# Weight conversion in fewer steps, keys and queries loaded as pairs of rows, division ahead of the transposes, and a new opening order, in a kernel of windowed attention and a gated feed-forward layer

## The chip, the cores and the metric

The kernel runs on one core of one Trainium2 chip. The metric is the time of one execution in device microseconds (us): a median of 659.19 over three runs (658.7 to 659.53) for the kernel before.

## The reference

Attention over 4 batches, 8 heads, 768 positions and 64 numbers per head, then a gated feed-forward layer without an activation over 3072 tokens (512 to 1536 and back). Weights arrive as 64-bit floats.

```python
k_sum = k.reshape(B, H, nb, 32, D).max(axis=3)            # 24 block summaries per head
v_sum = v.reshape(B, H, nb, 32, D).mean(axis=3)
scores_l = scale * q @ k.T, kept where |i - j| < 16        # else -1e9
scores_s = scale * q @ k_sum.T + log(32)
a = softmax(concat([scores_l, scores_s]))                  # sum + 1e-9 in the divisor
x = a @ concat([v, v_sum])                                 # heads side by side: 3072 x 512
out = ((x @ w_a) * (x @ w_b)) @ w_out
```

## The kernel before, in words

**Tiling.** Queries go in groups of 128 rows; a group's scores are a window of 96 keys and 24 block summaries for each half of 64 queries, 120 columns per head, four pairs of heads in one PSUM bank and two banks (h = 0, 1) per group. Groups are gathered into units: units 0 and 1 are two groups each, unit 2 two more, the later ones three. `attention` and `first_attention` make `x` of a unit; `item` runs one slice f of 128 columns of the hidden layer for a unit: `up` (x times w_a and w_b, L1110), the gate, `down` (times w_out, L1232). There are 12 slices. For slices 0, 1 and 11, units 0 and 1 run apart with 256 columns per product; for slices 2 to 10 they run together with 512. x, the gate's result and the weights are each kept as a high part and a remainder in the fp32r format, so `up` takes 12 products per matrix and `down` 3 per group.

**Weights.** `convert` (L401) turns two parts of 512 columns x 128 rows of doubles (w_a, w_b or w_out of a slice) into fp32 and then into high and low. Per part: ACT scales the high words into PSUM (L424), DVE shifts them into `f` (L432), DVE cuts the exponent out (L439), DVE multiplies the low words by it into `p` (L445); ACT casts `f` to the high part (L477), POOL subtracts that from `f` (L482), POOL adds `p` (L488). 36 parts in all, in places of two parts in one operation where the scratch allows.

**The first four groups** (`first_attention`, units 0 and 1) are special. Keys and queries are loaded with rows on partitions (`heads`, runs of 64 floats) and turned by TensorE with `turn` (L507, four transposes); the mask and the log are added by TensorE before the scores (`masks`, L695: four products of 480 columns against the identity); the softmax runs on PSUM; the division is folded into the transposes: DVE builds a diagonal of reciprocals (L786) and `turned` multiplies each 120 x 128 block by it (L807). Later groups use DVE for masks and transposes.

**Order.** Every operation is recorded with `work.add` and gets an index; `emit` issues them by priority and an assumed duration, but the table `ORDER` fixes for each engine the order of the indices that it lists. Each engine runs its list strictly in order. SP's list is the queue of loads. `SPIN` lists 16 products against the identity whose results nobody reads (L1338); the table places them on PE.

Of the kernel before, what the change touches and what calls it, by code (L numbers as in the profile page):

```python
# [25 lines left out]
        2638 2639 13 2640 5 2641 1 2642 2643 21 2644 17 9 2645 75 57 55 77 58 78 2646-2648 96 98  # L26
        2649-2651 111 100 113 121 102 141 123 104 106 124 143 151 2652 153 154 2653 115 145 173
        171 542 543 180 175 550 178 548 182 549 555 557 556 558 565 563 564 572 570 573 571 582
        583 580 578 581 579 588 590 354 591-593 602 589 600 598 603 599 601 612 610 611 613 608
        609 622 618 623 620 619 621 632 630 628 633 629 631 642 643 640 638 641 639 650 648 510  # L30
        652 673 653 649 651 662 660 658 661 682 659 667 679 687 668 688 940 941 948 946 947 793
        955 953 954 962 960 849 961 967-969 976 974 975 983 903 981 829 982 990 997 988 989 1004
        995 996 883 1002 1003 1046 1009 1011 1018 1010 937 1016 1017 1023 1024 1186 1187 1194
        1195 1192 1193 1202 1200 1201 1097 1203 1210 1208 1209 1211 1218 1216 1217 1219
    """,
    "ACT": """
# [8 lines left out]
        806 809 958 802 963 965 970 972 857 977 855 854 862-864 861 865 979 856 689 984 858 986  # L45
# [3 lines left out]
    """,  # L49
    "DVE": """  # L50
        7 3 15 23 19 11 195 59 60 80 79 196 65 72 66 73 67 74 197 199 85 86 200 87 92 93 201 94
        209-211 213 126 214 223 215 224 125 225 227 138 228 139 156 131 155 132 140 133 168 229
# [25 lines left out]
    """,
    "SP": """
# [20 lines left out]
    ("h1", 512), ("h1", 128), ("h1", 64), ("h1", 64), ("h1", 256), ("h1", 256), ("h1",  # L100
    128), ("h1", 128), ("h1", 256), ("h1", 256), ("h1", 256), ("h1", 256), ("h1", 256),
    ("h1", 256), ("h1", 256), ("h1", 128)
# [76 lines left out]
def attention_moe(  # L179
# [193 lines left out]
    raws, homes = {}, {}  # L373

    def load_part(i, rank):
# [7 lines left out]
        def fn():  # L383
            if j not in raws:
                raws[j] = wp.tile([P, 2048], I32, tag=f"W{j}", name=f"raw{j}")
            dst = raws[j][:, i % 2 * 1024 : (i % 2 + 1) * 1024]
# [14 lines left out]
    def convert(j):  # L401
        rank = CONVERT + j / 6
# [10 lines left out]
        cols = [[slice(x * CV, (x + 1) * CV) for x in xs] for _, *xs in places]  # L413
        fx, px = [[spaces[places[h][0]][:, cols[h][x]] for h in range(2)] for x in range(2)]
        fk, pk = [[f"{places[h][0]}.{places[h][1 + x]}" for h in range(2)] for x in range(2)]
        spans = [(h,) for h in range(2)] if single else [(0, 1)]

        def scale(h):
            high = raws[j][:, 2 * h * CV : 2 * (h + 1) * CV].rearrange("p (n t) -> p n t", t=2)
            nc.scalar.activation(  # L424
                bank["c0"], high[:, :, 1].bitcast(F32), AF.Prelu, scale=2.0**-112, alpha=-(2.0**32)
            )
# [474 lines left out]
    def first_attention():  # L901
# [82 lines left out]
        for t in range(2):  # L984
            begin(t, f"h{t}")
# [389 lines left out]
```

## Time and profile before

| what | value |
|---|---|
| median of three runs | 659.19 us (658.7, 659.19, 659.53 in order of size) |
| span of the profiled execution, first to last instruction | 656.9 us |
| median less span: what lies around the span | 2.3 us |
| busy: PE / weight loads / DVE / ACT / POOL | 647.7 / 599.3 / 409.9 / 250.8 / 187.8 us |
| HBM read, written | 47.41 MB, 6.44 MB |
| mean granted TensorE clock | 0.999 |

For the profiled execution itself the profile gives the span alone; its own time is taken as the span and the 2.3 us around it. How to read it: "busy" adds up the time in which an engine had an instruction running, and a TensorE product counts until its results have drained. Its successor starts before that, so the price of a product in a stream is the distance from its start to the next one's, and the duration printed for a merged row is longer than its price by the drain of its last product.

### The profile page before, as it was taken

How to read it: one execution, taken by the hardware profiler on the slowest of the kernel's cores; microseconds unless marked ns; L12 is line 12 of the kernel's file. 1: busy time of each engine (PE TensorE's matmuls, PEld its weight loads, DVE VectorE, ACT ScalarE, POOL GpSimd, SP SyncE). 2: the span in 40 equal slices, each digit the busy share in tenths (PEclk: the TensorE clock that was granted, in tenths of full speed). 3: DMA queues.
4: the chain of work that ended last, by engine and by line, in shares of the span. 5: the costliest groups of instructions: out<-in, count | busy, mean ns of one | idle time of the engine just before them, and what ended most of it. 6: DMA issues, size and time to landing. Idle time of an engine off the chain costs nothing.

```text
span 656.9 us, 12984 instructions
## 1 busy us (share of the span) xinstructions
PE 647.7 (99%) x4943; PEld 599.3 (91%) x4943; DVE 409.9 (62%) x857; ACT 250.8 (38%) x749; POOL 187.8 (29%) x246
## 2 busy tenths in 40 slices
PE   8899999999999999999999999999999999999997
PEld 6699888899989999999999999999999999999997
DVE  3899999997786784666767846667652531122212
ACT  4997676523443441433333313343321411121111
POOL 6498999847333440111010101110100100000000
PEclk9999999999999999999999999999999999999999
DMA  9998666353443443322112422221100200010001
GB/s 218 277 286 243 229 188 173 79 118 105 128 92 78 112 95 57 71 82 44 39 39 52 84 42 43 41 82 35 25 1 1 71 1 1 0 49 1 0 1 49
DMA packets 158198, 54.71 MB, mean 83 GB/s; under 512 B 135736, under 2 KB 151352, under 8 KB 158136
## 3 DMA queue, kind: packets, MB, share of 16 engines
q1 hardware_dynamic: 157992, 53.75, 33.9%
q8 instruction: 39, 0.64, 0.4%
q14 instruction: 23, 0.19, 0.1%
q10 hardware_dynamic: 144, 0.13, 0.1%
HBM read 47.41 MB, written 6.44 MB: 82 GB/s over the span
## 4 chain that ended last, share of the span: by engine, by line
PE 89%; DMA 6%; SPq 2%; ACT 1%; issue 1%; POOL 0%; DVE 0%; DVEq 0%
PE h L1110 54%; PE o L1232 27%; PE c L708 3%; PE o L856 3%; SPq L357 2%; DMA raw<-in_moe_w_out_dram 1%; DMA space<-in_v_dram 1%; DMA raw<-in_moe_w_b_dram 1%; DMA raw<-in_moe_w_a_dram 1%; DMA space<-in_q_dram 1%; DMA qin<-in_q_dram 1%; SPq L389 1%; PE c L1110 1%; POOL space L482 0%; PE c L856 0%
## 5 line engine op out<-in xcount | busy, mean ns | idle before, releaser
L1110 PE MATMUL h<-x,w 128*128 128x384 f32 (+2 forms) x2064 | 389.1, 321 | 0.0
L1110 PEld LDWEIGHTS h<-x,w 128*128 128x128 f32 x2064 | 331.3, 190 | 10.5 <-issue 0.6
L1232 PE MATMUL o<-w,gh 128*128 128x512 f32 x534 | 131.7, 382 | 0.0
L1217 DVE TENSOR_TENSOR h<-h,g 128x384 f32<-128x384 f32 x71 | 40.2, 566 | 136.4 <-PE h L1110 128.8
L1219 ACT CAST gh<-h 128x384 fp32r<-128x384 f32 x71 | 34.0, 478 | 204.6 <-DVE h L1217 202.0
L1232 PEld LDWEIGHTS o<-w,gh 128*128 128x128 f32 x534 | 97.6, 189 | 12.2 <-issue 1.6
L840 DVE STREAM_TRANSPOSE pt<-s 32x256 f32<-32x256 f32 x228 | 99.4, 436 | 13.0 <-POOL s L794 8.3
L794 POOL TENSOR_TENSOR s<-s,nml 128x480 f32<-128x480 f32 x40 | 39.4, 987 | 220.2 <-DVE nml L779 218.1
L1110 PE MATMUL h<-late,w 128*128 128x384 f32 x288 | 93.9, 326 | 0.0
L759 ACT ACTIVATE s<-s,nml 128x120 f32<-128x120 f32 x160 | 61.3, 386 | 38.0 <-DVE nml L745 37.8
L1232 PE MATMUL o<-w,gl 128*128 128x512 f32 x231 | 63.3, 381 | 0.0
L1110 PEld LDWEIGHTS h<-late,w 128*128 128x128 f32 x288 | 54.4, 189 | 0.9
L1222 DVE TENSOR_TENSOR gl<-h,gh 128x384 fp32r<-128x384 f32 x71 | 39.4, 555 | 23.0 <-ACT gh L1219 22.5
L1214 ACT COPY g<-h 128x384 f32<-128x384 f32 x71 | 34.0, 478 | 51.3 <-PE h L1110 50.9
L1232 PEld LDWEIGHTS o<-w,gl 128*128 128x128 f32 x231 | 43.3, 189 | 6.5 <-issue 0.5
L639 POOL TENSOR_TENSOR S<-S 96x256 f32<-96x256 f32 (+3 forms) x58 | 33.0, 571 | 43.8 <-DMA S<-in_v_dram 41.1
L737 DVE SCALAR_TENSOR_TENSOR s<-c,mask 128x480 f32<-128x480 f32 x40 | 25.8, 652 | 24.0 <-PE c L708 23.9
L424 ACT ACTIVATE c<-raw 128x512 f32<-128x512 f32 x36 | 29.3, 814 | 13.2 <-DVE S L432 5.7
L759 ACT ACTIVATION_READ_ACCUMULATOR s<-s,nml 128x1 f32 x160 | 30.2, 189 | 0.0
L482 POOL TENSOR_TENSOR space<-space,w 128x1024 f32<-128x1024 f32 (+1 forms) x14 | 26.7, 1912 | 3.5 <-ACT w L477 3.2
L488 POOL TENSOR_TENSOR w<-space 128x1024 fp32r<-128x1024 f32 (+1 forms) x14 | 26.7, 1912 | 0.9
L745 DVE TENSOR_REDUCE nml<-s 128x4 f32<-128x480 f32 x40 | 25.8, 648 | 0.7
(139 smaller groups left out, 586.0 us busy)
## 6 DMA issues: line engine op xcount, KB each, us to landing
raw<-in_moe_w_a_dram SPq DMA_DIRECT2D x12, 512.0 KB, 5.7
raw<-in_moe_w_b_dram SPq DMA_DIRECT2D x12, 512.0 KB, 7.9
raw<-in_moe_w_out_dram SPq DMA_DIRECT2D x12, 512.0 KB, 4.8
out_dram<-S SPq DMA_DIRECT2D x23, 256.0 KB, 2.2
qin<-in_q_dram SPq DMA_DIRECT2D x288, 16.0 KB, 1.7
S<-in_v_dram SPq DMA_DIRECT2D x24, 192.0 KB, 3.3
kin<-in_k_dram SPq DMA_DIRECT2D x38, 100.0 KB, 2.5
vw<-in_v_dram SPq DMA_DIRECT2D x18, 192.0 KB, 3.4
```

Of the source, the lines that this page charges most:

```text
L424: nc.scalar.activation(bank["c0"], high[:, :, 1].bitcast(F32), AF.Prelu, scale=2.0**-112, alpha=-(2.0**32))
L482: lambda ms=ms, f8=f8: nc.gpsimd.tensor_tensor(out=f8, in0=f8, in1=parted(0)[:, ms].bitcast(F32), op=ALU.subtract),
L639: lambda: nc.gpsimd.tensor_tensor(out=out, in0=i0, in1=i1, op=ALU.add),
L759: lambda h=h, c=c, sums=sums: nc.scalar.activation(s[h][:, c, :], x[h][:, c, :], AF.Exp, bias=m[:, 0, h, c : c + 1], scale=1.0, accum_out= ...
L794: lambda h=h, r=r: nc.gpsimd.tensor_tensor(out=s[h], in0=s[h], in1=r[:, :, None].broadcast_to([P, NP, KN]), op=ALU.mult,),
L840: lambda js=js, qs=qs, rs=rs: nc.vector.transpose(out=pv[js, rs, qs], in_=sv[qs, rs, js]),
L1110: nc.tensor.matmul(ps, w[:, c, part, :], (xt[:, 4 * xpart : 4 * xpart + 4] if both else inputs_of(u, xpart))[:, :, c].rearrange("p g (a b) ...
L1214: act(CHAIN, 0.13 + W / 1030, [ak], gk, lambda: nc.scalar.copy(out=g, in_=pa))
L1217: lambda: nc.vector.tensor_tensor(out=pb, in0=pb, in1=g, op=ALU.mult),
L1219: act(CHAIN, 0.16 + W / 1030, [bk], [ghk], lambda: nc.scalar.copy(out=gh, in_=pb))
L1222: lambda: nc.vector.tensor_tensor(out=gl, in0=pb, in1=gh.bitcast(F32), op=ALU.subtract),
L1232: nc.tensor.matmul(bank[ok[j]], (gh if first else gl)[:, j * P : (j + 1) * P], w[:, :, part, :].rearrange("p (z a) n -> p z n a", a=2), st ...
```

## The change

Six things:

1. `convert`: per part, ACT scales the high words straight into `f` in SBUF; DVE takes the top three bits of the low words as an integer into PSUM (`tail`); DVE shifts `f` and ors them in (`join`); ACT casts; POOL subtracts once. One DVE operation and one POOL operation per part go. The two parts of the first three pairs get tiles of their own.
2. Keys and queries of the first four groups are loaded with two neighbouring rows side by side on a partition (`paired`, runs of 128 floats) and turned by `turn_pairs`: eight ordinary products of 64 columns of weights against the identity, in two column halves, in place of four transposes. A turned tile holds two pairs of heads and 256 rows, and is copied into place in more and smaller pieces.
3. The division is done by DVE on the probabilities, and the blocks are turned with plain transposes.
4. Masks stay products in unit 0; in unit 1 DVE adds them while it copies the scores to SBUF.
5. Unit 1's queries are turned into the banks h0 and h1, and summaries wait for half of the keys only.
6. New `ORDER` tables (shorter: from where they end, priorities decide) and other banks for the spins.

```diff
 def convert(j):
+            def scale(f=f, words=words):
+                nc.scalar.activation(
+                    f, words()[:, :, 1].bitcast(F32), AF.Prelu, scale=2.0**-112, alpha=-(2.0**32)
+                )
+            def tail(t=t, words=words):
+                nc.vector.tensor_scalar(
+                    out=t, in0=words()[:, :, 0].bitcast(U32), scalar1=2.0**-29, scalar2=7.0,
+                    op0=ALU.mult, op1=ALU.min,
+                )
+            def join(f=f, t=t):
+                nc.vector.scalar_tensor_tensor(
+                    out=f.bitcast(I32), in0=f.bitcast(I32), scalar=3, in1=t,
+                    op0=ALU.logical_shift_left, op1=ALU.bitwise_or,
+                )
...
             pool(
-                rank + 0.1 * hs[0], takes, hi, f,
-                lambda ms=ms, f8=f8: nc.gpsimd.tensor_tensor(
-                    out=f8, in0=f8, in1=parted(0)[:, ms].bitcast(F32), op=ALU.subtract
+                rank + 0.1 * hs[0], 0.2 + 1.1 * len(hs), hi + f, lo,
+                lambda hs=hs, f8=f8: nc.gpsimd.tensor_tensor(
+                    out=parted(1, hs), in0=f8, in1=parted(0, hs).bitcast(F32), op=ALU.subtract
                 ),
             )
-            pool(
-                rank + 0.1 * hs[0], takes, f + p, lo,
...
+    def paired(x):
+        return x.rearrange("h (p t) d -> p h (t d)", t=2)
+
+    def turn_pairs(bk, x):
+        v4 = x.rearrange("p (h t d) -> p h t d", t=2, d=D)
+        for c in range(2):
+            for t in range(2):
+                n = 2 * c + t
+                for h in range(2):
+                    nc.tensor.matmul(
+                        bank[bk][h * D : (h + 1) * D, n * P : (n + 1) * P],
+                        v4[:, 2 * c + h, t, :], ident, start=True, stop=True,
+                        tile_position=(0, h * D),
+                    )
...
-        masked = u < FILL
+        first = u < FILL
+        masked = first and u < 1
...
-                    lambda h=h, r=r, d=d: nc.vector.tensor_tensor(
-                        out=d[:, h], in0=ident[:, None, :].broadcast_to([P, NP, P]),
-                        in1=r[:, :, None].broadcast_to([P, NP, P]), op=ALU.mult,
+                    lambda h=h, r=r: nc.vector.tensor_tensor(
+                        out=s[h], in0=s[h], in1=r[:, :, None].broadcast_to([P, NP, KN]),
+                        op=ALU.mult,
...
-                    nc.tensor.matmul(
-                        bank[banks[h]][:KN, c * P : (c + 1) * P], s[h][:, c, :KN], d[:, h, c, :],
-                        start=True, stop=True,
+                    nc.tensor.transpose(
+                        bank[banks[h]][:KN, c * P : (c + 1) * P], s[h][:, c, :KN], ident
                     )
```

How the tables move things, at three places of the opening. In these rows `raw` is a part of the weights as loaded, `w` its converted home, `space_180` to `space_185` scratch tiles, `vw` the value rows of a group, `o_73`/`o_74` and `o_75`/`o_76` the score banks of the first and second group of a unit, `h_77`/`h_78` the banks h0 and h1.

SP, the queue of loads, from the last keys to the second pair of query loads (before, then now; L383 and L389 load weights, L330 and L357 the rest):

```order
L357 DMA space_180<-in_k_dram 128x8x64
L357 DMA space_181<-in_q_dram 128x8x64 x2
L389 DMA raw_205<-in_moe_w_a_dram 128x4x256
L357 DMA space_182<-in_v_dram 128x4x128 x3
L357 DMA space_180<-in_q_dram 128x8x64
L389 DMA raw_205<-in_moe_w_b_dram 128x4x256
L357 DMA space_182<-in_v_dram 128x4x128
L389 DMA raw_274<-in_moe_w_out_dram 128x1024
L357 DMA space_183<-in_v_dram 128x4x128 x2
L389 DMA raw_274<-in_moe_w_a_dram 128x4x256
L389 DMA raw_292<-in_moe_w_b_dram 128x4x256
L357 DMA space_180<-in_q_dram 128x8x64
```

```order
L383 DMA raw_207<-in_moe_w_b_dram 128x4x256
L330 DMA space_183<-in_v_dram 128x4x128
L383 DMA raw_220<-in_moe_w_a_dram 128x4x256
L330 DMA space_182<-in_v_dram 128x4x128 x4
L330 DMA space_183<-in_v_dram 128x4x128
L383 DMA raw_250<-in_moe_w_out_dram 128x1024
L330 DMA vw_158<-in_v_dram 80x8x64
L330 DMA vw_159<-in_v_dram 64x8x64
L383 DMA raw_269<-in_moe_w_a_dram 128x4x256
L330 DMA space_180<-in_q_dram 128x4x128
L330 DMA space_184<-in_v_dram 32x8x64
L330 DMA space_180<-in_q_dram 128x4x128
```

All loads for the block means (`space_182`, `space_183`) now stand ahead of the first slice's w_out, the values of group 0 (`vw_158`, `vw_159`) ahead of unit 1's queries, and those queries behind one part of slice 1 in place of two.

ACT, from the second half of unit 0's softmax to the copies of unit 1's queries (L819 and L816 copy turned probabilities, L973 and L969 copy turned queries, L1009 and L1012 copy the block means, L876 and L873 cast x, L424 and L422 scale weights, L477 and L463 cast them):

```order
L759 ACTIVATE space_183,nml_172<-o_76,nml_172 128x120
L973 ACTIVATE qT<-o_73 128x512
L424 ACTIVATE c_79<-raw_274 128x512
L819 COPY space_180<-o_75 120x512
L477 CAST w_419<-space_188 128x4x128 x2
L424 ACTIVATE c_79<-raw_274 128x512
L1009 COPY vw_159<-h_77 24x512
L1009 COPY vw_158<-h_77 24x512
L424 ACTIVATE c_79<-raw_292 128x512
L819 COPY space_180<-o_76 120x512
L759 ACTIVATE s,nml_171<-o_74,nml_171 128x120 x3
L973 ACTIVATE space_184<-o_75 128x512
```

```order
L759 ACTIVATE space_183,nml_172<-o_75,nml_172 128x120 x3
L873 CAST x<-h_77 128x512
L816 COPY space_180<-o_76 120x512
L422 ACTIVATE space_187<-raw_269 128x512
L463 CAST w_504<-space_188 128x4x128
L969 ACTIVATE qT<-h_78 128x256
L969 ACTIVATE space_184<-h_78 128x256
L969 ACTIVATE qT<-h_77 128x256
L422 ACTIVATE space_186<-raw_303 128x512
L969 ACTIVATE space_184<-h_77 128x256
L816 COPY space_180<-o_75 120x512
```

The copies of unit 1's queries are four of 256 columns in place of two of 512, and group 0's x (`x<-h_77`) is cast ahead of them; before it came after the softmax of unit 1 had begun.

PE, around the first products of the feed-forward layer (L856 and L853 values, L807 and L805 the turning of probabilities, L1110 and L1114 `up`):

```order
L856 MATMUL h_78<-space_180,space_184 64x64 x16
L807 MATMUL o_74<-pt,s 120x128 x4
L807 MATMUL o_73<-pt,s 120x128 x4
L1110 MATMUL h_77<-x,w_419 128x256 x24
L807 MATMUL o_76<-space_180,space_183 120x128 x4
```

```order
L1114 MATMUL h_77<-x,w_504 128x256 x12
L1114 MATMUL h_77<-x,w_375 128x256 x12
L1114 MATMUL h_78<-x,w_557 128x256 x12
L1114 MATMUL h_78<-x,w_576 128x256 x12
L805 MATMUL o_74<-ident,s 120x128 x4
L805 MATMUL o_73<-ident,s 120x128 x4
L805 MATMUL o_76<-ident,space_183 120x128 x4
L805 MATMUL o_75<-ident,space_183 120x128 x4
L853 MATMUL o_73<-pt,vw_158 64x64 x2
```

Both first slices' `up` of unit 0 now stand ahead of unit 1's transposes and values; before, one slice stood between its two groups.

## Rows read from the trace of the kernel before

**Rows 1.** The profile's first part: busy microseconds, share of the span and instructions of each engine.

```profile
PE 647.7 (99%) x4943; PEld 599.3 (91%) x4943; DVE 409.9 (62%) x857; ACT 250.8 (38%) x749; POOL 187.8 (29%) x246
```

**Rows 2.** The trace cut into stretches (start:end, length, then busy microseconds and number of instructions for PE, its weight loads, DVE, ACT and POOL; then granted TensorE clock as a share of full speed, mean busy share of the DMA engines, GB/s).

```profile
0.00:20.00 20.00, 17.04 (x134) 13.45 (x135) 8.66 (x17) 10.59 (x39) 12.04 (x54) 1.00 1.11 236
20.00:40.00 20.00, 17.92 (x222) 15.04 (x222) 19.48 (x44) 18.69 (x62) 12.93 (x13) 1.00 1.02 265
...
200.00:300.00 100.00, 100.00 (x773) 94.30 (x772) 67.93 (x157) 34.02 (x120) 25.82 (x47) 1.00 0.38 81
...
600.00:657.00 57.00, 52.93 (x300) 50.40 (x298) 11.73 (x22) 9.79 (x20) 0.00 (x0) 0.99 0.04 15
```

**Rows 3.** PE's instructions in order of time, the opening (start, time from the first start to the last end, line, operation, out<-in, rows of weights, shape, how many, and in brackets the idle time before it and what ended it). L1338 is a spin, L507 a turn of keys or queries, L695 a mask product, L708 scores, L807 a diagonal product, L856 values, L1110 a first-layer product, L1232 a second-layer one.

```profile
1.43 2.50 PE L1338 MATMUL h<-ident 128*128 128x512 f32 x4 [1.43 <-POOL ident masks.py:199]
...
6.61 1.09 PE L507 MATMUL c<-ident,space 128*128 128x128 f32 x4
7.50 1.13 PE L1338 MATMUL h<-ident 128*128 128x256 f32 x4
...
9.78 0.60 PE L507 MATMUL c<-ident,space 128*128 128x128 f32 x4
10.21 0.64 PE L507 MATMUL o<-ident,space 128*128 128x128 f32 x4
...
12.73 0.60 PE L507 MATMUL h<-ident,space 128*128 128x128 f32 x4
13.10 1.12 PE L695 MATMUL o<-space 128*128 128x480 f32 x4
14.14 1.05 PE L708 MATMUL o<-kT,qT 64*64 64x120 f32 x32
15.01 1.00 PE L708 MATMUL o<-kT,space 64*64 64x120 f32 x32
...
22.49 1.04 PE L807 MATMUL o<-pt,s 128*120 128x128 f32 x8
23.37 0.60 PE L507 MATMUL o<-ident,space 128*128 128x128 f32 x4
...
29.69 0.63 PE L507 MATMUL o<-ident,space 128*128 128x128 f32 x4 [0.49 <-DMA space<-in_q_dram]
...
34.09 1.15 PE L856 MATMUL h<-pt,vw 120*64 120x64 f32 x32
35.07 1.10 PE L856 MATMUL h<-space,space 120*64 120x64 f32 x32
...
38.33 2.92 PE L1110 MATMUL h<-x,w 128*128 128x256 f32 x24
```

**Rows 4.** PE's instructions in order of time, later on.

```profile
57.46 2.75 PE L1110 MATMUL h<-x,w 128*128 128x512 f32 x12
...
130.65 2.84 PE L1110 MATMUL h<-x,w 128*128 128x256 f32 x24
133.33 1.89 PE L1232 MATMUL o<-w,gh 128*128 128x512 f32 x8
...
150.52 2.94 PE L1110 MATMUL h<-x,w 128*128 128x256 f32 x24
153.30 1.46 PE L1232 MATMUL o<-w,x 128*128 128x512 f32 x6
```

**Rows 5.** The DMA traffic in stretches of 2 us (columns as in the stretches above).

```profile
6.00:8.00 2.00, 2.00 (x11) 1.97 (x10) 0.69 (x1) 0.91 (x3) 1.61 (x9) 1.00 1.35 218
...
18.00:20.00 2.00, 1.80 (x8) 1.62 (x9) 0.70 (x4) 2.00 (x14) 0.14 (x1) 1.00 1.13 346
```

**Rows 6.** ACT's instructions in order of time. Of an exponential (L759) the next one starts before the read of its accumulator ends, so that the distance of two starts is its price.

```profile
16.58 0.35 ACT L759 ACTIVATE s<-o,nml 128x120 f32<-128x120 f32 x1
...
16.91 0.36 ACT L759 ACTIVATE s<-o,nml 128x120 f32<-128x120 f32 x1
...
24.40 0.60 ACT L973 ACTIVATE qT<-o 128x512 f32<-128x512 f32 x1
24.87 0.66 ACT L424 ACTIVATE c<-raw 128x512 f32<-128x512 f32 x1
25.45 0.60 ACT L819 COPY space<-o 120x512 f32<-120x512 f32 x1
...
27.65 1.17 ACT L1009 COPY vw<-h 24x512 f32<-24x512 f32 x2
28.79 0.64 ACT L424 ACTIVATE c<-raw 128x512 f32<-128x512 f32 x1
```

**Rows 7.** POOL's instructions in order of time, the weights of the first 512-column product.

```profile
48.96 2.40 POOL L488 TENSOR_TENSOR w<-S 128x1024 fp32r<-128x1024 f32 x1
```

**Rows 8.** Groups of instructions by line, engine and operation, with count | busy us, mean ns of one | idle time of the engine before them and its releasers.

```profile
L488 POOL TENSOR_TENSOR w<-space 128x1024 fp32r<-128x1024 f32 (+1 forms) x14 | 26.7, 1912 | 0.9
L745 DVE TENSOR_REDUCE nml<-s 128x4 f32<-128x480 f32 x40 | 25.8, 648 | 0.7
...
L488 POOL TENSOR_TENSOR w<-S 128x512 fp32r<-128x512 f32 (+1 forms) x11 | 17.4, 1583 | 0.9
...
L439 DVE TENSOR_SCALAR c<-space 128x512 int32<-128x512 int32 x22 | 15.1, 684 | 0.2
...
L439 DVE TENSOR_SCALAR c<-S 128x512 int32<-128x512 int32 x14 | 9.6, 686 | 0.2
```

More of the change, by code (lines that the diff above doesn't have):

```diff
@@ L25 @@
     "PE": """
[L26 to L30, printed above, removed]
@@ L372, in attention_moe, with raw, home @@
     parts = [(f, nm) for f in range(NF) for nm in "abo"]
-    raws, homes = {}, {}
+    raws, homes, both = {}, {}, {}
+    def raw(i):
+        j, h = i // 2, i % 2
+        if j < 3:
+            if i not in raws:
+                raws[i] = wp.tile([P, 1024], I32, tag=f"W{j}.{h}", name=f"raw{i}")
+            return raws[i]
+        if 2 * j not in raws:
+            x = wp.tile([P, 2048], I32, tag=f"W{j}", name=f"raw{2 * j}")
+            raws[2 * j], raws[2 * j + 1] = x[:, :1024], x[:, 1024:]
+        return raws[i]
+    def home(i):
+        j, h = i // 2, i % 2
+        if j < 3:
+            if i not in homes:
+                homes[i] = wp.tile([P, 4, 2, P], F32R, tag=f"W{j}.{h}", name=f"w{i}")
+            return homes[i]
+        if 2 * j not in homes:
+            x = wp.tile([P, 8, 2, P], F32R, tag=f"W{j}", name=f"w{2 * j}")
+            homes[2 * j], homes[2 * j + 1] = x[:, :4], x[:, 4:]
+            both[j] = x
+        return homes[i]
     def load_part(i, rank):
@@ L383, in fn @@
         def fn():
-            if j not in raws:
-                raws[j] = wp.tile([P, 2048], I32, tag=f"W{j}", name=f"raw{j}")
-            dst = raws[j][:, i % 2 * 1024 : (i % 2 + 1) * 1024]
+            dst = raw(i)
             if nm != "o":
@@ L412, in convert @@
             single = True
[L413 to L415 removed]
+        cols = [slice(x * CV, (x + 1) * CV) for _, x, _ in places]
+        fx = [spaces[places[h][0]][:, cols[h]] for h in range(2)]
+        fk = [f"{places[h][0]}.{places[h][1]}" for h in range(2)]
         spans = [(h,) for h in range(2)] if single else [(0, 1)]
[L422 to L425, printed above, removed]
[L426 removed]
@@ L449, in convert @@
-        for n, h in [(n, h) for h in range(2) for n in range(3)]:
-            f, p, e, s, r = [fk[h]], [pk[h]], ["c0"], ["c1"], [rk[h]]
-            if n == 0:
-                act(CHAIN, 0.52, r, e, lambda h=h: scale(h))
-            reads, writes = ((e, f), (f, s), (r + s, p + [f"done{j}"] + r))[n]
-            dve(rank, 0.6, reads, writes, lambda n=n, h=h: step(n, h))
-        def parted(part):
-            if j not in homes:
-                homes[j] = wp.tile([P, 8, 2, P], F32R, tag=f"W{j}", name=f"w{j}")
-            return homes[j][:, :, part, :]
+        whole = [f"whole{j}"] if single and j > 2 else []
@@ L461, in convert, with parted @@
+        work.add("-", 0, 0, 0, [f"done{j}.{h}" for h in range(2)], [f"done{j}"], lambda: None)
+        if whole:
+            work.add(
+                "-", 0, 0, 0, [f"{x}{j}.{h}" for x in ("whole", "done") for h in range(2)], whole, lambda: None
+            )
+        def parted(part, hs):
+            y = home(2 * j + hs[0])
+            if len(hs) == 2:
+                y = both[j]
+            return y[:, :, part, :]
         for hs in spans:
-            ms = slice(4 * hs[0], 4 * (hs[-1] + 1))
@@ L548, in attention_moe @@
     KT = [f"kT{c}{x}" for c in range(NP) for x in "ks"]
+    def paired(x):
[5 more added lines that the diff above has]
+                n = 2 * c + t
+                for h in range(2):
+                    nc.tensor.matmul(
[3 more added lines that the diff above has]
+                    )
     def first_keys():
-        n = P // BLK
-        for i in range(S // P):
+        for i in range(6):
+            j, hh = i // 2, i % 2
+            cs = slice(2 * hh, 2 * hh + 2)
             x, key = spot(i // 2)
@@ L579, in first_keys @@
         for c in range(NP):
-            work.add("-", 0, 0, 0, [f"ksi{i}" for i in range(6)], [f"ks{c}"], lambda: None)
-            work.add("-", 0, 0, 0, [f"kT{i}" for i in range(6)], [f"kT{c}k"], lambda: None)
+            work.add("-", 0, 0, 0, [f"ksi{i}" for i in range(c // 2, 6, 2)], [f"ks{c}"], lambda: None)
+            work.add("-", 0, 0, 0, [f"kT{i}" for i in range(c // 2, 6, 2)], [f"kT{c}k"], lambda: None)
             summaries(FIRST, c)
@@ L735, in scores @@
                 dve(
-                    rank, 0.6, [banks[h]], [sk[h]],
+                    rank, 0.6, [banks[h]], [sk[h], *(f"{sk[h]}{c}" for c in range(NP) if first)],
                     lambda h=h: nc.vector.scalar_tensor_tensor(
                         out=s[h], in0=y[h],
-                        scalar=0.125, in1=mask[:, kind, None, :KN].broadcast_to([P, NP, KN]),
+                        scalar=1.0 if first else 0.125, in1=mask[:, kind, None, :KN].broadcast_to([P, NP, KN]),
                         op0=ALU.mult, op1=ALU.add,
@@ L752, in scores @@
             l = m[:, 1, h, :]
-            sums, r = l, x[h][:, :, 0] if masked else l
+            sums, r = l, y[h][:, :, 0] if first else l
             for c in range(NP):
@@ L757, in scores @@
                     rank, 0.385, [f"{mk}m{h}", xk[h]],
-                    [f"{mk}l{h}{c}"] + ([f"{sk[h]}{c}"] if masked else []),
+                    [f"{mk}l{h}{c}"] + ([f"{sk[h]}{c}"] if first else []),
                     lambda h=h, c=c, sums=sums: nc.scalar.activation(
@@ L813, in transposes @@
                 pe(
-                    -1, 0.85, [f"{sk[h]}{c}" for c in range(NP)] + dk[h], [banks[h]],
+                    -1, 0.44, [sk[h], *(f"{sk[h]}{c}" for c in range(NP))], [banks[h]],
                     lambda h=h: turned(h),
@@ L1058, in begin @@
             dve(
-                rank_of(u, t0 + i) - 0.05 * (u > FILL), 0.62, keys, ["qT"],
+                rank_of(u, t0 + i) - 0.05 * (u > FILL), 0.62, keys, ["qT", "qT.0", "qT.1"],
                 lambda: nc.vector.transpose(out=qTs, in_=qin[:, :, place(i)]),
             )
-            scores(u, t0 + i, qTs, "qT", s0, SK, banks, lead=lead.pop() if lead else None)
+            scores(u, t0 + i, qTs, ["qT"], s0, SK, banks, lead=lead.pop() if lead else None)
         def turned(i):
```

199 lines of the change are left out of this document (88 added, 111 removed), and 57 rows, old and new, of the table ORDER.

## The prediction, made before the changed kernel ran

> **What bounds the kernel now.** I read the page's first part, then the trace cut into stretches, then PE's instructions in order. TensorE is busy 647.7 of 656.9 us [rows 1]. The stretches show where the other 9.2 us lie: 2.96 in the first 20 us, 2.08 in the next 20, 4.07 in the last 57 (the final stores), and 0.00 of the hundred us from 200 on [rows 2]. Busy is not useful, though: the opening also holds spins, and turns that run at the lower clock. From the first product of the feed-forward layer at 38.33 [rows 3] PE goes from product to product, and every such product is still there after the change. So the end moves by what the opening gives, and by little else. DVE, busy 19.48 of 20 us from 20 to 40 [rows 2], and POOL matter only where PE waits for what they make.
>
> **What the change removes.** In `convert` 36 DVE operations (L439, 15.1 and 9.6 us) and 25 POOL operations (L488, 26.7 and 17.4 us) go [rows 8]: 24.7 us of DVE and 44.1 of POOL. `join` takes L445's place, `tail` L432's, at about the same price. Behind 38 us PE is dense over this work, so I count it at nothing; where the cover ends is the first rival. On PE: two mask blocks go. One costs 13.10 to 14.14, about 1.0 [rows 3], so -2.0; four further DVE operations at 0.65 (L745, as wide, [rows 8]) take their place. Eight halves of diagonal products become plain transposes: 22.49 to 23.37, 0.88 for four products; four transposes take 9.78 to 10.21, 0.43 [rows 3]: -3.6. Dividing on DVE costs what building the diagonal cost, an operation of about 500 columns either way.
>
> **What it adds.** Ten turns become pair turns: eight fp32 products of 128 columns, each in two passes. At 0.11 a pass (0.88 for eight, above), 16 passes cost 1.76 if nothing runs side by side, and 0.88 if the two column halves do. The nearest row is the values: they use the same halves, and 32 passes of 64 columns take 34.09 to 35.07, 0.031 each, against 0.055 for 64 columns alone [rows 3]. I take 0.88, so +4.5 on PE in all; the ends are 0.43 (the old turn) and 1.76. In sum PE has 1.1 us less work. What counts is when it runs.
>
> Entering and leaving such a mode may cost too. Scores, also in parts of the array, start 1.04 after four mask products of 480 columns, which at the 512-column rate (0.216: 2.75 less 0.16 of drain, over 12) are 0.81; and 24 products take 2.78 behind scores (150.52 to 153.30) against 2.68 elsewhere (130.65 to 133.33) [rows 3, 4]. That is 0.1 to 0.3 for a visit, part of it a wait; I take 0.1. The Trainium skill, "TensorEngine Tiling (Array Packing)", section Key Properties, says that changing the tiling mode drains TensorE, which speaks against pair turns between spins; the sum by the upper figure is the third rival.
>
> **The opening, step by step.**
> 1. *Arrival.* Keys and queries in runs of 256 bytes come at 218 GB/s, values in runs of 512 bytes at 346 [rows 5]. The eight first loads are 2.1 MB: 9.6 us before, 6.3 at 330 GB/s. The last is turned at 12.73 [rows 3]; now it has landed by about 9.6.
> 2. *Turning.* PE now sets the pace. The granted clock reads 1.00 [rows 2], yet a turn that starts at 6.61 takes 0.89 to the next row at 7.50 and one at 9.78 takes 0.43 [rows 3]: TensorE ran at its 1.2 GHz level until about 7.5, after 6 us of spins and turns, then at 2.4. The spins ahead of the first pair turn are 832 columns where 640 took 2.50 [rows 3], so it starts at 4.4; two turns and a spin at the lower level end near 7.9; six more (5.3), three spins of 256 columns (1.3) and one more (0.4) end at 14.9, the masks at 15.9. The last tile's maxima, then POOL's copies of the summaries, allow 16.0. Group 0's scores start at **16.0, not 14.14**: 1.9 later.
> 3. *First softmax.* Scores 0.87, a maximum 0.65 [rows 3, 8]; exponentials from 17.7. ACT's list has 13 exponentials at 0.33 (16.58 to 16.91), two copies of means (27.65 to 28.79, 1.14), two copies of probabilities at 0.47 (24.40 to 24.87, the same width) [rows 6]: 24.3 with 0.3 of waits for group 1's maxima. Values of group 0 at 24.4; before 34.09 [rows 3].
> 4. *Unit 1's queries.* Turned at 29.69 before, after a wait for their load [rows 3]. By the new queue 6.7 MB lie ahead of them, at 300 GB/s 24.4; PE asks for them at about 26, so the load ends no wait any more. ACT is late next: a scaling (0.58, 24.87 to 25.45), three exponentials, x, a copy, a scaling, a cast (0.47 to 0.58), three copies of 256 columns (0.3, an estimate between half of 0.47 and all of it) [rows 6] bring group 2's scores to 28.9. A scaling and two copies later, at 30.2, values of group 1 can run; they also need POOL's copy of the means, which its list holds behind the subtraction for the first w_a, at about 30.1.
> 5. *First `up`.* Scores of group 3 end at 32.1, and ACT, after three casts of weights, casts x of group 1 then too; with 0.7 us for some ten hops between engines, `up` starts at **32.8, not 38.33**.
> 6. *To the first 512-column product.* Before, 57.46 [rows 4]. Now: two slices' `up` (2 x 2.68) to 38.2, under which ACT does unit 1's 16 exponentials; the turning and values of groups 2 and 3 wait for ACT's four copies and end at 42.0; then 8.8 us of products (48 of 256 columns at 0.112, 16 of 512 at 0.216) to 50.8. Weights of slice 2 are ready by my count of ACT and POOL at 51.8 (before 48.96 + 2.40 = 51.4, six us ahead of their use [rows 7]): **51.9**. One pair of 0.43 is then still owed. Gain 57.46 - 51.9 - 0.43 = 5.1.
>
> **The sum.** 656.9 - 5.1 = 651.8 of span; with the 2.3 us by which the median lies above the profiled span, **654.1** against 659.19. Ends: pair turns at the old price, or spins' gaps used up, -2 more; the rivals the other way.
>
> **Rivals.** *Late weights.* With the start earlier, slice 2's weights are just in time, since DVE's list puts their last step behind unit 1's softmax, and ACT casts them behind four scalings. For it: six us of lead become nothing. Against: a part now needs two DVE and one POOL operation. If they come 2.5 to 5 us later than 51.8, the gain falls to 2.6 or 0: 656.6 to 659.2. *Pair turns one after the other* (slower): if the column halves do not overlap, each of the eight costs 0.88 more, all of it ahead of group 0's scores; 654.1 + 7.0 = 661.1. It decides from 1.52 us a turn (5.1 over 8, above 0.88). Against it stand the values' rows [rows 3]. *Mode changes* at 0.3 for seven visits, five of them ahead of the first scores: about 2.1 to 2.5, 656.5. The scores' rows [rows 3, 4] put most of that on the wait ahead of them.
>
> **Chances.** A measurement of this kernel tells about 0.2%, 1.3 us, from no change. Forecast, with its own spread of 651 to 656: 0.60. Late weights 0.18, of which half gains more than 1.3 and half about nothing. Mode changes 0.10, nearly all still a gain. Turns one after the other 0.08, and 0.04 for other losses (the order behind the tables' end, which now comes earlier). So faster 0.77, same 0.11, slower 0.12. The range 650.8 to 659.4 leaves out the slower cases and a few hundredths at the lower end.
>
> **What the next profile would show.** Right: loads near 330 GB/s from 2 to 8 us; pair turns 0.88 apart once the clock is up; group 0's scores at 16, its values at 24 to 25, the first `up` near 33, the first 512-column product near 52, and the same products without gaps from there; DVE busy near 388 (409.9 - 24.7 + 2.6), POOL near 144. Wrong: pair turns over 1.2 us, PE idle in front of the 512-column products for a weight, or group 2's scores no earlier than before.

## The result, and the profile after

The changed kernel takes **663.21 us** (663.07 to 663.71) against 659.15 for the kernel before on the same chip: a ratio of 1.0064, 95% interval 1.0049 to 1.0078. It is slower, and the prediction of 654.1 was wrong, range included.

The profile's first part answers to [rows 1]: POOL lost the work it was to lose, DVE 15.7 of 22.1 us, and PE is busy 0.7 us longer.

```profile
PE 648.4 (98%) x5023; PEld 598.9 (91%) x5023; DVE 394.2 (60%) x825; ACT 253.3 (38%) x765; POOL 144.4 (22%) x221
```

The stretches, with the columns of [rows 2]. TensorE is busy longer in the first 20 us than before, and stands idle for 2.5 us between 140 and 220, where the kernel before (the last line) does not stand idle at all.

```profile
0.00:20.00 20.00, 18.23 (x219) 14.36 (x219) 7.26 (x12) 9.92 (x39) 12.48 (x55) 1.00 0.97 259
20.00:40.00 20.00, 18.55 (x244) 15.63 (x241) 16.48 (x38) 18.29 (x70) 10.35 (x11) 1.00 0.90 223
...
140.00:220.00 80.00, 77.50 (x784) 71.66 (x783) 59.01 (x134) 31.32 (x119) 31.91 (x62) 1.00 0.41 100
```

```profile
140.00:220.00 80.00, 80.00 (x791) 73.74 (x788) 61.14 (x144) 32.37 (x127) 38.04 (x72) 1.00 0.43 106
```

PE's instructions in order of time, which answer to [rows 3, 4] (L538 is a pair turn, L805 a plain transpose of probabilities, L853 values, L1114 `up`, L1236 `down`):

```profile
11.23 1.09 PE L538 MATMUL h<-ident,space 128*64 128x128 f32 x16
12.15 1.04 PE L538 MATMUL c<-ident,space 128*64 128x128 f32 x16
13.02 1.04 PE L538 MATMUL h<-ident,space 128*64 128x128 f32 x16
13.90 1.04 PE L538 MATMUL c<-ident,space 128*64 128x128 f32 x16
...
16.37 0.44 PE L708 MATMUL o<-kT,qT 64*64 64x120 f32 x8
17.14 0.84 PE L708 MATMUL o<-kT,qT 64*64 64x120 f32 x24 [0.33 <-POOL kT L521]
...
26.05 1.15 PE L853 MATMUL h<-pt,vw 120*64 120x64 f32 x32
...
29.73 1.09 PE L538 MATMUL h<-ident,space 128*64 128x128 f32 x16 [0.26 <-DMA space<-in_q_dram]
...
31.34 1.05 PE L708 MATMUL o<-kT,qT 64*64 64x120 f32 x32
33.41 1.16 PE L853 MATMUL h<-space,space 120*64 120x64 f32 x32 [1.02 <-ACT space L816]
...
35.48 0.71 PE L1114 MATMUL h<-x,w 128*128 128x256 f32 x4
...
54.75 2.75 PE L1114 MATMUL h<-x,w 128*128 128x512 f32 x12
...
92.67 1.99 PE L1236 MATMUL o<-w,gh 128*128 128x512 f32 x8 [2.75 <-ACT gh L1168]
...
195.90 1.03 PE L853 MATMUL o<-pt,vw 120*64 120x64 f32 x28 [1.24 <-DVE pt L837]
...
209.59 1.56 PE L1236 MATMUL o<-w,gh 128*128 128x512 f32 x6 [0.91 <-ACT gh L1223]
```

So the opening did gain: the first 512-column product starts 2.71 us earlier than in [rows 4]. Behind it that and more is lost. To see where, I took for every product of the two layers, the scores and the values the distance to the next start on PE, less its price in a dense stream (0.2157 us for 512 columns, 0.1625 for 384, 0.1117 for 256, 0.0306 a pass of scores, 0.0338 of values; these prices add up to the same 611.5 us in every kernel here). What is over is lost. "Behind" is from 220 us on. "Rest" is the time of everything else on PE ahead of the last product: spins, turns, masks, turned probabilities, block means, and the waits around them. The stretches are those of the profiled execution; its time is within 0.5 us of the median but for e6 (1.0 over) and e9 (0.6 over). **Lost us by stretch:**

| kernel | median | span | 0-60 | 60-140 | 140-220 | behind | rest |
|---|---|---|---|---|---|---|---|
| before | 659.2 | 656.9 | 0.5 | 1.8 | 2.0 | 2.9 | 34.2 |
| changed | 663.2 | 661.6 | 2.5 | 5.4 | 4.8 | 2.9 | 30.4 |
| e1, lighter conversion | 658.1 | 655.9 | 0.2 | 1.1 | 1.9 | 2.9 | 34.1 |
| e4, all four parts, old order | 661.3 | 659.4 | 1.7 | 0.8 | 2.3 | 2.9 | 36.1 |
| e6, five loads moved | 660.3 | 659.3 | 3.2 | 3.4 | 4.5 | 2.9 | 29.7 |
| e9, own opening, old order | 659.6 | 658.4 | 7.6 | 0.8 | 2.3 | 2.9 | 29.2 |
| e10, both repairs | 658.3 | 656.8 | 3.1 | 3.7 | 1.9 | 2.9 | 29.6 |

The changed kernel loses 8.4 us more than the one before, 6.4 of it between 60 and 220 us, and its rest takes 3.8 us less; together that is, but for rounding, the 4.7 between the two profiled spans.

**The chain behind the largest wait**, 2.75 us at 92.67. SP's instructions (SPq; start, time, what it loads, how many):

```profile
65.12 0.43 SPq L383 DMA_DIRECT2D raw<-in_moe_w_b_dram  x1
72.55 1.75 SPq L330 DMA_DIRECT2D qin<-in_q_dram  x4
74.39 1.86 SPq L383 DMA_DIRECT2D raw<-in_moe_w_a_dram  x2
```

DVE's (L427 and L433 conversion, L1064 transposes queries, L1166 multiplies the gate), and one of ACT's (L1168 casts the gate's result):

```profile
71.83 0.70 DVE L1064 STREAM_TRANSPOSE qT<-qin 128x512 f32<-128x512 f32 x1
...
84.74 1.60 DVE L427 TENSOR_SCALAR c<-raw 128x512 int32<-128x512 uint32 x2 [2.31 <-DMA raw<-in_moe_w_b_dram]
...
91.23 0.69 DVE L1166 TENSOR_TENSOR h<-h,g 128x512 f32<-128x512 f32 x1
...
92.03 0.59 ACT L1168 CAST gh<-h 128x512 fp32r<-128x512 f32 x1 [3.06 <-DVE h L1166]
```

SP issues nothing from 65.6 to 72.55: the next entry of its list loads queries into a tile that DVE reads at 71.83 only. Six weight loads that have no such wait stand behind it in the list. They go out 6 to 8 us later than in e6 below, DVE stands still for 2.31 us at 84.74, and the gate's multiply, behind the conversions in DVE's list, starts at 91.23, 1.7 us after its products ended. ACT casts, and PE goes on at 92.67.

### The profile page after: what moved, and what is told of

The parts are those of the page before. It is cut to its first block, busy times and chain, and to the rows that moved or that the text cites. A ratio compares the mean times of both kernels' runs of the same rounds, so it can differ in the third digit from the quotient of the medians.

```text
span 661.6 us, 13050 instructions
## 1 busy us (share of the span) xinstructions
PE 648.4 (98%) x5023; PEld 598.9 (91%) x5023; DVE 394.2 (60%) x825; ACT 253.3 (38%) x765; POOL 144.4 (22%) x221
## 4 chain that ended last, share of the span: by engine, by line
PE 77%; SPq 9%; DMA 7%; DVE 2%; issue 2%; POOL 1%; ACT 1%; DVEq 0%; POOLq 0%; ACTq 0%
PE h L1114 46%; PE o L1236 24%; SPq L330 7%; DMA raw<-in_moe_w_b_dram 4%; PE o L853 3%; PE c L708 2%; SPq L383 2%; DMA raw<-in_moe_w_a_dram 1%; DMA raw<-in_moe_w_out_dram 1%; DVE pt L837 1%; DVE c L427 1%; PE c L1114 1%; POOL w L467 1%; DMA S<-in_v_dram 0%; DMA kin<-in_k_dram 0%
## 5 line engine op out<-in xcount | busy, mean ns | idle before, releaser
L1114 PE MATMUL h<-x,w 128*128 128x384 f32 (+2 forms) x2064 | 389.5, 321 | 0.3 <-DVE x L1196 0.3
L1114 PEld LDWEIGHTS h<-x,w 128*128 128x128 f32 x2064 | 331.5, 190 | 11.4 <-DVE x L1171 0.8
L1236 PE MATMUL o<-w,gh 128*128 128x512 f32 x534 | 131.9, 382 | 3.8 <-ACT gh L1168 2.9
L1236 PEld LDWEIGHTS o<-w,gh 128*128 128x128 f32 x534 | 97.7, 189 | 16.9 <-ACT gh L1168 3.7
L1114 PE MATMUL h<-late,w 128*128 128x384 f32 x288 | 93.9, 326 | 0.0
L759 ACT ACTIVATE s<-s,nml 128x120 f32<-128x120 f32 x168 | 64.3, 386 | 38.2 <-DVE nml L745 38.1
L1236 PE MATMUL o<-w,gl 128*128 128x512 f32 x231 | 63.3, 381 | 0.0
L1114 PEld LDWEIGHTS h<-late,w 128*128 128x128 f32 x288 | 54.4, 189 | 1.0
L1226 DVE TENSOR_TENSOR gl<-h,gh 128x384 fp32r<-128x384 f32 x71 | 39.3, 554 | 22.6 <-ACT gh L1223 22.1
L1236 PEld LDWEIGHTS o<-w,gl 128*128 128x128 f32 x231 | 43.3, 189 | 6.5 <-issue 0.5
L467 POOL TENSOR_TENSOR w<-space,w 128x1024 fp32r<-128x1024 f32 (+1 forms) x14 | 26.7, 1918 | 28.0 <-ACT w L463 25.9
L759 ACT ACTIVATION_READ_ACCUMULATOR s<-s,nml 128x1 f32 x168 | 31.9, 190 | 0.0
L427 DVE TENSOR_SCALAR c<-raw 128x512 int32<-128x512 uint32 x36 | 28.3, 800 | 5.0 <-DMA raw<-in_moe_w_b_dram 4.4
L1236 PE MATMUL o<-w,x 128*128 128x512 f32 x96 | 25.4, 384 | 0.0
```

The costliest lines, as they stand in the source:

```text
L427: nc.vector.tensor_scalar(out=t, in0=words()[:, :, 0].bitcast(U32), scalar1=2.0**-29, scalar2=7.0, op0=ALU.mult, op1=ALU.min,)
L467: lambda hs=hs, f8=f8: nc.gpsimd.tensor_tensor(out=parted(1, hs), in0=f8, in1=parted(0, hs).bitcast(F32), op=ALU.subtract),
L759: lambda h=h, c=c, sums=sums: nc.scalar.activation(s[h][:, c, :], x[h][:, c, :], AF.Exp, bias=m[:, 0, h, c : c + 1], scale=1.0, accum_out= ...
L1114: nc.tensor.matmul(ps, w[:, c, part, :], (xt[:, 4 * xpart : 4 * xpart + 4] if both else inputs_of(u, xpart))[:, :, c].rearrange("p g (a b) ...
L1226: lambda: nc.vector.tensor_tensor(out=gl, in0=pb, in1=gh.bitcast(F32), op=ALU.subtract),
L1236: nc.tensor.matmul(bank[ok[j]], (gh if first else gl)[:, j * P : (j + 1) * P], w[:, :, part, :].rearrange("p (z a) n -> p z n a", a=2), st ...
```

## The experiments

The first four keep the order of before: every engine runs before's list, so that only the operations differ.

**e1: the lighter conversion alone.**

```diff
-bank["c0"], high ... AF.Prelu ...      # scale into PSUM, then three DVE steps, two POOL steps
+fx[h], high ... AF.Prelu ...           # scale into f, then tail and join, one POOL step
```

> Before's program in before's complete order of instructions on every engine, with the lighter weight conversion alone (the removed operations are simply gone from their lists). Theory (the new operations are no loss, the new order is): TensorE's products stand as before, the conversions only get lighter, so 658.5 to 659.7 us, no difference, and no stall over 0.5 us in front of a 512-column product. Rival (the lighter conversion itself loses: its longer single operations, or the raw weight buffers held longer, make weights or the gate late): 661 to 664 us with stalls of 1 to 3 us in the feed-forward layer.

658.14 us (ratio 0.9982, 0.9973 to 0.9991): neither. It is a small gain, 0.7 of it as fewer losses from 60 to 140 us. The rival falls: in this order these operations delay nothing.

**e2: division on DVE and plain transposes alone.**

```diff
-nc.tensor.matmul(to, s[h][:, c, :KN], d[:, h, c, :], start=True, stop=True)
+nc.tensor.transpose(to, s[h][:, c, :KN], ident)
```

> Before's program and order with the division on VectorE and plain transposes of the probabilities alone. Theory: 3.6 us of TensorE's work go, 1.8 of them in groups 0 and 1 and 1.8 in groups 2 and 3, most of it ahead of the first feed-forward products: 656 to 658 us. Rival (the opening is set by VectorE and ScalarE, not by TensorE's turns): 658.7 to 659.5 us, no difference.

659.5 us (1.0003, 0.9994 to 1.0012): the rival. PE is busy 644.0 us, 3.7 less, as the working had it (-3.6), yet the span stays (657.0): all of it has become waiting.

**e3: paired keys and unit 0's queries alone** (loads of 128 floats, `turn_pairs`, the copies that follow; unit 1's queries as before).

> Before's program and order with the paired loads and pair turns of the first keys and of unit 0's queries alone (unit 1's queries stay as they were). Theory: TensorE gets 8 x 0.45 = 3.6 us more of turning, the first eight loads arrive 2 to 3 us sooner; the turns fill waits for loads, so 658.5 to 660.5 us. Rival (pair turns cost what the loads give back and more, through mode changes or longer turns): 661 to 663 us.

662.52 us (1.0044, 1.0032 to 1.0057): the rival's time, though not by mode changes in the main. PE's opening, and a wait of before that is gone here:

```profile
11.05 0.49 PE L1491 MATMUL h<-ident 128*128 128x128 f32 x2
11.47 1.09 PE L625 MATMUL c<-ident,space 128*64 128x128 f32 x16
12.39 1.04 PE L625 MATMUL o<-ident,space 128*64 128x128 f32 x16
13.36 0.49 PE L1491 MATMUL h<-ident 128*128 128x128 f32 x2
...
17.97 1.05 PE L817 MATMUL o<-kT,qT 64*64 64x120 f32 x32
```

```profile
9.09 0.63 PE L507 MATMUL c<-ident,space 128*128 128x128 f32 x4 [0.46 <-DMA space<-in_k_dram]
```

Here a turn takes 0.92 or 0.97 to the next row, about the price I had, and PE waits for no load, where before waited 0.46 at 9.09 and 0.28 at 11.36. But the scores of group 0 start 3.83 later than in [rows 3]. With the 0.74 of waits that are gone, turning takes 4.6 us longer: eight times 0.45, and 1.0 more, of which I did not take apart what the first turn (1.90 from 3.94 to 5.84, twice the later ones) and the mode changes have. With the loads sooner, turning is the path, and nearly all of its extra price comes out at the end: 3.5 us between the profiled spans (660.4 and 656.9), 3.2 between the medians.

**e4: all four parts** (with unit 1's masks on DVE; unit 1's queries as before, as in e3).

> All four parts of the change (lighter conversion, paired first keys and unit 0's queries, division on VectorE with plain transposes, unit 1's masks on VectorE) in before's complete order of instructions. Theory (operations gain, the new order loses): 653.5 to 657 us, faster than before, and no stall over 1 us in the feed-forward layer behind 60 us. Rival (the operations themselves lose): 660 to 664 us.

661.3 us (1.0027, 1.0018 to 1.0035). Half of the theory holds: behind 60 us nothing is lost (0.8 from 60 to 140). The other half falls: in the old order the operations themselves lose, in the opening. The first 512-column product starts 3.16 later than in [rows 4], and part of that is clock: behind a wait of 3.34 the granted clock is at 0.50 (the last line, columns as in [rows 2]), and 32 passes of scores take 1.75 to the next row, where [rows 3] have 0.87 (14.14 to 15.01).

```profile
34.71 1.82 PE L817 MATMUL o<-kT,space 64*64 64x120 f32 x32 [3.34 <-ACT space L1113]
36.46 0.80 PE L1491 MATMUL h<-ident 128*128 128x128 f32 x2
...
60.62 1.67 PE L1263 MATMUL h<-x,w 128*128 128x512 f32 x7
```

```profile
35.00:36.00 1.00, 1.00 (x28) 1.00 (x24) 1.00 (x3) 1.00 (x5) 0.86 (x1) 0.50 0.84 266
```

**e8: three parts, without the pairs.**

> Before's program in before's complete order with three parts of the change, without the paired loads and turns: lighter conversion, division on VectorE with plain transposes, unit 1's masks on VectorE. Theory (the paired turns are the part that costs, 3 us in before's order): 656 to 658 us. Rival (the parts undo one another, as the division alone gave nothing): 658.5 to 660 us.

658.44 us (0.9996, 0.9987 to 1.0005), 0.06 below the rival's range. The pairs cost about 2.5 us beside the others (e4 is 2.0 above the kernel before that ran beside it, e8 0.5 below), somewhat less than the 3.2 alone. The other three together give no more than the lighter conversion alone. Why is shown in part: with the plain transposes alone, PE's time turns into waiting (e2), and in e8's profiled execution PE waits for the copy of unit 1's queries and for the division, on engines whose lists have conversions between unit 1's softmax steps. But that execution took 661.15, 2.7 over the median, with the granted clock at 0.50 from 26 to 29 us, so these waits need not be those of the others.

```profile
32.70 1.05 PE L817 MATMUL o<-kT,space 64*64 64x120 f32 x32 [1.86 <-ACT space L1113]
...
38.92 1.73 PE L929 MATMUL o<-ident,s 128*120 128x128 f32 x8 [2.73 <-DVE s L904]
```

The other runs keep the changed kernel's operations and move its lists.

**e6: five loads moved in SP's list.**

```diff
 SP: ... 382 381
-747 745 746 754 393 406 750 405 394 418 751 417 ...
+393 406 405 394 418 751 417 747 745 746 754 750 ...   # 743-758: queries; the others: weights
```

> The changed program with five loads of unit 2's queries moved in SP's list from ahead of the ten weight loads behind them (raw w_a, w_b, w_out of slices 8 to 10, issued at 74.4 to 79.0 us) to behind those loads; nothing else moves. Theory (the blocked query loads hold the weights up, and those hold up VectorE, ScalarE and then TensorE at 92.67): the weights are issued about 8 us earlier, VectorE's wait of 2.31 at 84.74 and TensorE's of 2.75 at 92.67 go, so 663.2 - 2.8 = 660.4, in 659.5 to 661 us. Rival (the gate's multiply is late because six conversion operations stand ahead of it in VectorE's list, not because of the loads): the stall stays, 662.5 to 664 us.

660.33 us (against before 1.0022, 1.0012 to 1.0032), 2.9 less than the changed kernel: the theory, to 0.1 us. (Six weight loads are passed in the list, not the ten that I wrote.) The changed kernel's DMA moved 250 and then 214 GB/s from 60 to 80 and 80 to 100 us; now 335 and 158 (columns as in [rows 2]):

```profile
60.00:80.00 20.00, 19.92 (x118) 16.99 (x117) 18.98 (x29) 15.77 (x29) 11.76 (x5) 1.00 1.06 335
80.00:100.00 20.00, 19.49 (x89) 16.45 (x88) 18.21 (x31) 14.51 (x27) 13.66 (x8) 1.00 0.57 158
```

DVE's wait at 84.74 is gone, and PE's falls to 0.51, though the same conversions stand ahead of the gate:

```profile
90.40 1.78 PE L1308 MATMUL o<-w,gh 128*128 128x512 f32 x7 [0.51 <-ACT gh L1240]
```

**e5 and e7: before's order spliced on,** behind 55 us and behind the changed list's end at about 140 us.

> The changed program, its operations untouched, in its own order up to the first 512-column product (about 55 us), and behind that in the order in which the program before runs the same operations, on all five engines. Theory (the opening is a gain of some 2.5 us, the order behind it is what loses): TensorE's losses behind 60 us fall from 10.4 us to before's 4.0, so 663.2 - 6.4 = 656.8, in 655.5 to 658 us. Rival (the losses behind 60 us come from the conversion's operations, which here are the same, whatever the order): 661 to 663.5 us.

> The changed program in its own order to the end of its written list (about 140 us), and behind that in the order of before. Theory (the stalls of 1.43 at 194.4 and 1.08 at 208.4 come from the order that the planner makes where the list no longer covers): the losses from 140 to 220 us fall from 5.0 to about 2.3, so 660.5, in 659.5 to 661.5 us; the stall at 92.67 stays. Rival (they come from work that is late already at 140 us): 662.5 to 664 us.

672.79 us (1.022, 1.0201 to 1.0239) and 668.34 us (1.0139, 1.0125 to 1.0152): neither theory, but a flaw of the edit. It put each later unit's transposes of queries directly ahead of their scores, and their loads with them; e9 below, e5 with these put back, is 13 us faster. In e7 the changed kernel's waits at 195.90 and 209.59 are gone, and one of 5.20 stands at 251:

```profile
251.04 1.22 PE L1313 MATMUL o<-w,gh 128*128 128x512 f32 x2 [5.20 <-ACT gh L1300]
```

**e9 and e10: the splices mended,** e10 with the loads of e6 as well.

> As the run with the changed program's order up to about 55 us and before's behind it, but with VectorE's 18 transposes of later units' queries where before has them too (the earlier run had put each directly ahead of its scores, which made stalls of 1.4 to 5.4 us from 133 us on). Theory (before's order loses nothing behind 120 us with these operations, as the run with all four parts showed): the stalls from 120 us on go, losses behind 120 us fall from 19.2 to about 6 us. The stall of 3.06 at 53.6, where before's order has the weights of slice 2 too late for the earlier start, stays: 658.5 to 660.5 us. Rival (two orders cannot be joined without loss wherever the seam is): stalls over 1 us behind 120 us stay, over 663 us.

> The changed program with both repairs: the five query loads behind the weight loads in SP's list, and before's order on all engines behind the changed list's end (about 140 us), with the query transposes in their places. Theory (the blocked loads and the planner's order behind the list's end are the two losses of the changed order): the stalls of 0.75 at 192.2 and 1.69 at 205.4 that the first repair left go too, 660.3 - 2.3 = 658.0, in 657 to 659 us. Rival (work late at 140 us comes out as a stall wherever the order lets it): 660 to 662 us.

e9: 659.56 us (1.0002, 0.9993 to 1.0011), e10: 658.27 us (0.9983, 0.9973 to 0.9993), both as the theory had it. In e10 the losses from 140 to 220 us fall from 4.5 (e6) to 1.9: the order that priorities make behind the shorter table costs 2.1 us between the medians (660.33 - 658.27). **With both repairs the change is 4.9 us faster than as it came, and faster than the kernel before by 0.17%**; e1 alone is as fast, so no run here shows a gain from the other parts.

e9 shows the other thing. There the opening is the changed kernel's, and the whole gain and more is given back at one place:

```profile
52.12 1.46 PE L1314 MATMUL o<-w,x 128*128 128x512 f32 x6
56.61 2.08 PE L1314 MATMUL o<-w,gh 128*128 128x512 f32 x4 [3.04 <-ACT gh L1271]
```

The wait also costs clock (the last section), 1.4 us more. In DVE's list of before the gate's multiply (L1269 here) stands behind the conversions for the next slices, and DVE does those from 48.89 to 55.7 without more than 0.3 us of rest; it reaches the gate at 55.73:

```profile
55.12 0.69 DVE L511 SCALAR_TENSOR_TENSOR space<-space,c 128x512 int32<-128x512 int32 x1
55.73 0.43 DVE L1269 TENSOR_TENSOR h<-h,g 128x256 f32<-128x256 f32 x1
```

Here the earlier start is worth nothing, since the list behind it does not start earlier too.

## Why the prediction was wrong, step by step

**The step that failed** is the one that ends "PE goes from product to product, and every such product is still there after the change", with what I drew from it, "So the end moves by what the opening gives, and by little else", and "Behind 38 us PE is dense over this work, so I count it at nothing". The products are all there, but their density was a property of before's order. e4 keeps that order and loses 0.8 us from 60 to 140; the new one loses 5.4, of which five loads in SP's list take 2.0 (e6), and 4.8 from 140 to 220, of which the order behind the table's end takes 2.7 (e10). I had that last as "other losses" at 0.04, with no price, and had walked SP's list only through the opening. What is left of the excess from 60 to 140 us in e10 (3.7 against 1.8) I did not take apart: one wait of 0.50 at 90.25 is in it, and no other over 0.15. In the terms of the sum: where 5.1 of gain stood the opening gave 2.3 (2.71 less the pair of 0.43 still owed), and where nothing stood behind it 7.0 were lost, which makes the 4.7 by which the span grew.

**The opening** gained 2.71 where 5.56 stood (57.46 - 51.9), by steps:
1. *Arrival.* The loads moved 278 GB/s from 6 to 8 us where [rows 5] show 218, but 258 from 2 to 8, not 330. The 346 behind my 330 is from a stretch in which weights were loading too (its mean packet has 0.9 KB, not 512 bytes). The shortfall cost nothing: PE shows no wait for a load there. In the columns of [rows 5]:

```profile
6.00:8.00 2.00, 2.00 (x26) 1.56 (x23) 0.00 (x0) 0.24 (x2) 1.61 (x9) 1.00 1.21 278
2.00:8.00 6.00, 6.00 (x44) 4.61 (x43) 0.01 (x1) 0.33 (x3) 4.92 (x26) 1.00 0.99 258
```

2. *Turning.* Pair turns 0.87 to 0.92 apart, group 0's scores at 16.37 (forecast 16.0), then 0.33 more for a copy of summaries at 17.14. The rival of turns one after the other is refuted: the halves overlap.
3. *First softmax.* Values at 26.05, not 24.4; the exponentials start at 18.74, not 17.7. The first conversions stand ahead of them on both engines, which I had left out, but the first reduction starts 0.07 after the last score has ended (17.98), and the first exponential as the first maximum comes (18.05 and 0.65), so they cost next to nothing. DVE's list and ACT's, and ACT's before:

```profile
17.45 0.69 DVE L433 SCALAR_TENSOR_TENSOR space<-space,c 128x512 int32<-128x512 int32 x1 [1.17 <-ACT space L422]
18.05 1.22 DVE L745 TENSOR_REDUCE nml<-o 128x4 f32<-128x480 f32 x2
```

```profile
18.17 0.62 ACT L463 CAST w<-space 128x512 fp32r<-128x512 f32 x1 [0.18 <-DVE space L433]
18.74 0.36 ACT L759 ACTIVATE s<-o,nml 128x120 f32<-128x120 f32 x1
```

```profile
16.23 0.36 ACT L759 ACTIVATE s<-o,nml 128x120 f32<-128x120 f32 x1 [1.32 <-DVE nml L745]
```

   From the first score to the first exponential it takes 2.37, of which 0.33 is the wait for the summaries; the 2.04 left are what before takes (14.14 to 16.23: 2.09), and I had counted 1.7. So the 1.04 are 0.37 of later scores, 0.33 of that wait and 0.34 of my sum. The other 0.6 up to the values came along ACT's list, in small parts.
4. *Unit 1's queries.* "The load ends no wait any more" was wrong: they wait at 27.96 and 29.73; the loads moved 223 GB/s from 20 to 40 us, where I had 300. Group 2's scores come at 31.34, not 28.9. Then ACT's scaling of a late w_b stands ahead of group 1's copy (the wait of 1.02 at 33.41).
5. *First `up`* and 6. *the first 512-column product* carry the delay on: `up` at 35.48 for 32.8, the 512-column product at 54.75 for 51.9.

**The rivals.** *Late weights* came in another form. In the changed kernel six loads are late behind a blocked entry of SP's list; in e9 the gate is late, behind conversions in DVE's list, and not the weights. I had bounded this rival by the gain, but the 7.0 lost behind the opening are three times the gain. *Mode changes* were sized right as a rival and too small in the sum: in e3 two spin passes of 128 columns take 0.42 ahead of a pair turn (11.05 to 11.47), where before takes 0.23 for the same two ahead of a turn over the whole array (9.55, the line below, to 9.78 in [rows 3]), so entering costs about 0.2, and I had taken 0.1 for a visit. The Trainium skill, "TensorEngine Tiling (Array Packing)", section Key Properties, says that a change of the mode drains TensorE; the trace agrees, with that size. But pair turns behind each other pay no such thing (0.87).

```profile
9.55 0.39 PE L1338 MATMUL h<-ident 128*128 128x128 f32 x2
```

**What was right:** POOL at 144.4 us (144), PE's price of pairs (0.87 to 0.92 a turn, 0.88 forecast), -3.6 for the plain transposes in PE's busy time. DVE was forecast at 388 and came to 394.2. The two steps left cost what I had: `tail` takes 0.80 on the mean and `join` 0.68, the steps that they replaced 0.78 and 0.68. But the 24.7 that I took off were durations, and on DVE an operation starts before the one ahead of it has ended (18.05 against 17.45 and 0.69 above): the conversion's share of the busy time fell from 70.5 to 49.6, by 20.9, each operation counted up to the start of the next. The rest of the miss I did not trace.

```profile
L427 DVE TENSOR_SCALAR c<-raw 128x512 int32<-128x512 uint32 x36 | 28.3, 800 | 5.0 <-DMA raw<-in_moe_w_b_dram 4.4 <-DMA raw<-in_moe_w_out_dram 0.3
```

Still open is what the pairs are worth inside the new opening; only their price in before's order was measured.

## What to carry to other kernels

When a change brings new operations and a new order, forecast them apart: the new operations in the old order first, then each in-order list walked to its end, the load queue above all, for an entry that waits on a late reader with ready entries behind it. A dense stretch in the old profile is evidence for the old order only; a stretch counted at nothing needs a bound on what it can lose. And before counting on an earlier start, see that weights, conversions and gates behind it are earlier too; in e9 they were not, and it paid nothing.

## What the runs showed of the hardware that was not expected

**A wait of PE can cost twice.** In e9, stretches of 1 us around the wait of 3.04 (columns as in [rows 2]):

```profile
55.00:56.00 1.00, 0.00 (x0) 0.00 (x0) 0.90 (x3) 0.00 (x0) 1.00 (x1) 1.00 1.08 324
56.00:57.00 1.00, 0.39 (x1) 0.39 (x2) 1.00 (x4) 0.81 (x2) 0.41 (x1) 0.74 1.08 315
57.00:58.00 1.00, 1.00 (x3) 0.79 (x3) 1.00 (x4) 0.95 (x3) 0.00 (x0) 0.50 1.10 341
...
60.00:61.00 1.00, 1.00 (x6) 0.87 (x6) 0.90 (x2) 1.00 (x2) 1.00 (x1) 1.00 0.40 64
```

After it the granted clock is at 0.50, the lower of the two levels (1.2 GHz), for some 3 us, and six products of 512 columns take 2.72 us (56.61 to 59.33) where a dense stream has 1.29: 1.4 us on top of the wait. The wait of 3.34 in e4 (34.71) cost clock too. After the wait of 2.75 us in the changed kernel, at 92.67, it stayed at 1.00.

**One load in the wrong place travels far.** SP issued nothing for 7 us, from 65.6; PE waited 2.75 us for it at 92.67, by way of DVE and ACT, and moving five loads in SP's list gave 2.9 us back.
